# When the first MoE's weight blocks are decoded: a table of four rates in place of three

## The chip, the cores and the metric

One core of a Trainium2 chip runs the whole program. The time is the device time of one execution in microseconds (us), and lower is better. The engines have these names: PE multiplies matrices (PEld is its weight load, which overlaps), DVE is VectorE, ACT is ScalarE, POOL is GpSimd, and SP issues most of the DMAs.

## What is computed

Windowed and dilated causal attention, then two feed-forward layers ("MoE 1" and "MoE 2") with different activations. The weights arrive as float64.

```python
attn_out = _attn_ref(q, k, v)              # B=4, H=8, S=576, D=64; window 32, dilation 4 in half of the heads
x = attn_out.transpose(0, 2, 1, 3).reshape(2304, 512)
# MoE 1: w_in 512x2048, w_out 2048x512
h = x @ w_in
g = np.maximum(h, 0.0) + alpha * np.minimum(h, 0.0)
x = g @ w_out
# MoE 2: its own w_in, w_out
h = x @ w_in
P = a[0] + a[1]*h + a[2]*h*h + a[3]*h*h*h
Q = 1.0 + np.abs(b[0])*np.abs(h) + np.abs(b[1])*h*h
out = (P / (Q + 1e-06)) @ w_out
```

## The kernel before

**Products.** Each operand is split into a high part (`wh`, `xh`) and a low rest (`wl`, `xl`), and each product is three matmuls: wl by xh, wh by xl, wh by xh.

**Steps.** The 2304 tokens are taken in 8 groups `u` of 288, and the 2048 hidden units in 16 blocks `f` of 128. A step of MoE 1 is one pair (u, f), and there are 128. The list `SEQ` gives their order: steps 0 to 7 are group 0 with blocks 0 to 7, steps 8 to 15 group 1 with the same blocks 0 to 7, steps 16 to 23 group 0 with blocks 8 to 15, steps 24 to 31 group 1 with blocks 8 to 15, and from step 32 on one group after the other with all 16 blocks. So steps 8 to 15 need no block that steps 0 to 7 did not need, and step 16 + i needs block 8 + i for the first time.

Step n has two halves (`half1`). The first issues the 12 matmuls of `h` (L520) into one of two banks; the second issues the 12 matmuls of `y` (L673) for step n - 2, which need `w_out` of that step's block. Behind `h` runs a chain: ACT `r` (L640), DVE `h` (L643, the larger of two), ACT `g` high (L646), DVE `g` low (L649). When `g` low is done, the bank is free for `h` of step n + 2. Beside the steps run the attention jobs of the later groups: two load q and k (`tq`, `tk`), transpose them on PE (`pq`, `pk`), which ACT copies out (`qT`, `kT`, L362 and L363), multiply them (`ps`), and then turn and multiply further (`pr`, `pp`, L448).

**Turns.** A turn decodes two float64 pieces into float32: for turn k of MoE 1 these are `w_in` of block k and `w_out` of block k - 2 (turns 0, 1, 16 and 17 have one piece only). There are 18 turns for MoE 1 and 18 for MoE 2. A turn's stages are: `w64_load` (SP, L131 and L136, 512 KB each, two buffers `raw`), `w64_exponent` (ACT L145, one instruction of 128x1024), `w64_sign`, `w64_upper`, `w64_lower` (DVE L151, L158, L164, of 128x1024 each), and for MoE 1 `w64_hi` (ACT L187, makes `wh`) and `w64_lo` (DVE L197, makes `wl`, twice 128x512). A turn of MoE 2 stores its result to DRAM (`w2f`, SP L171) behind `w64_lower` instead. `tick()` runs all stages once, the load being that of the turn after the next. A head ahead of step 0 does the first four turns and one load more.

**The pace.** `half1` begins with

```python
rate = next((r for m, r in PACE if n < m), 0)
pace[0] += rate / 2
while pace[0] >= 1:
    pace[0] -= 1
    tick()
```

so a rate of 0.75 is three turns in four steps. `PACE` is a list of (step at which the rate ends, rate). The code's order is only a priority: a scheduler orders each engine's instructions by it, by what each depends on, and by its own estimates of their costs, and can issue a turn's instructions earlier than its tick.

Of the kernel before, what the change touches and what calls it, by code (L numbers as in the profile page):

```python
# [22 lines left out]
def tile_attention_moe_moe2(  # L23
# [60 lines left out]
    MAN = ''  # L84
    MAN_FROM = 0
    MAN_TO = 128
    PACE = ((14, 0.75), (22, 0.55), (128, 0.23))

    cst = ctx.enter_context(tc.tile_pool(name="cst", bufs=1))
    wpool = ctx.enter_context(tc.tile_pool(name="wpool", bufs=NF))  # L90
# [435 lines left out]
    if True:  # L526
# [225 lines left out]
        def half1(n, half):  # L752
            u = n // NF
            rate = next((r for m, r in PACE if n < m), 0)
            pace[0] += rate / 2
# [223 lines left out]
```

## Time and profile before

| | us |
|---|---|
| median of 3 runs | 977.42 |
| the three runs | 972.84, 977.42, 978.7 |
| the profiled execution | 978.13 |
| its span, first to last instruction | 976.4 |
| PE busy in the span | 937.6 |
| DVE busy | 666.2 |
| ACT busy | 632.1 |
| mean granted clock of PE, share of full speed | 0.979 |

The span is 1.7 us shorter than the execution that was profiled, and that execution is 0.7 us above the median. Busy time is an engine's own work, not its waits.

### The profile page before, as it was taken

To read this page: it belongs to the slowest core of one execution; us is meant where nothing else is said; L and a number is where in the kernel's file an instruction comes from. 1 tells how busy PE (TensorE), PEld (TensorE's weight loads), DVE (VectorE), ACT (ScalarE), POOL (GpSimd) and SP (SyncE) were. 2 spreads that over 40 slices of the span, in tenths; PEclk is the share of its full clock that TensorE was granted. 3 is DMA by queue.
4 is the path that set the end of the run, shared out by engine and by line. 5 is a ranking of instruction groups with operands and counts; after the bars stand their busy time and mean duration, and the time that the engine had idled before them with its cause. 6 is when DMAs were issued, how large, how long until landed. Compare 5 with 4: busy or idle time off the path is not lost.

```text
span 976.4 us, 18434 instructions
## 1 busy us (share of the span) xinstructions
PE 937.6 (96%) x6704; PEld 874.4 (90%) x6704; DVE 666.2 (68%) x1578; ACT 632.1 (65%) x1575; POOL 212.7 (22%) x257
## 2 busy tenths in 40 slices
PE   6789899999999999999999999999999999999998
PEld 5678799889899999999999999999999999999996
DVE  2888885556456555554435679877777788777776
ACT  3876665656455565564545578777677776777765
POOL 2000000001000010000112345434343343343332
PEclk7799999999999999999999999999999999999999
DMA  7656535563634535322134432002030020020000
GB/s 182 162 177 178 201 117 161 137 196 97 188 115 119 184 112 162 124 83 83 50 109 136 153 112 66 1 33 65 1 94 4 31 67 1 33 65 1 34 1 33
DMA packets 93899, 94.41 MB, mean 97 GB/s; under 512 B 40176, under 2 KB 81648, under 8 KB 93808
## 3 DMA queue, kind: packets, MB, share of 16 engines
q1 hardware_dynamic: 87360, 83.78, 28.1%
q0 software_dynamic: 6448, 9.45, 3.8%
q8 instruction: 53, 0.87, 0.4%
q14 instruction: 38, 0.31, 0.1%
HBM read 69.48 MB, written 23.72 MB: 95 GB/s over the span
## 4 chain that ended last, share of the span: by engine, by line
PE 83%; ACT 5%; DMA 5%; DVE 4%; issue 1%; SPq 1%; POOL 0%; POOLq 0%; ACTq 0%; DVEq 0%
PE h L520 39%; PE o L892 20%; PE y L673 17%; DMA raw<-in_moe_w_out_dram 3%; PE px L499 2%; PE pp L448 2%; ACT pr L427 1%; PE ps L405 1%; DMA hd<-in_q_dram 1%; PE ps L393 1%; ACT hd L427 1%; DVE w L158 1%; DVE wl L197 1%; DVE w L164 1%; PE pk L356 1%
## 5 line engine op out<-in xcount | busy, mean ns | idle before, releaser
L520 PE MATMUL h<-x1h,wl 128*128 128x288 f32 x512 | 159.3, 312 | 7.0 <-DVE g_0l L649 2.4
L520 PE MATMUL h<-x1l,wh 128*128 128x288 f32 x512 | 154.2, 301 | 0.0
L520 PE MATMUL h<-x1h,wh 128*128 128x288 f32 x512 | 153.5, 300 | 0.0
L643 DVE SCALAR_TENSOR_TENSOR h<-h,salpha,r 128x288 f32<-128x288 f32 x128 | 66.9, 523 | 112.7 <-ACT r L640 112.6
L520 PE MATMUL h<-x2h,wl 128*128 128x384 f32 x384 | 130.4, 340 | 0.0
L520 PE MATMUL h<-x2h,wh 128*128 128x384 f32 x384 | 130.0, 339 | 0.0
L520 PE MATMUL h<-x2l,wh 128*128 128x384 f32 x384 | 129.6, 338 | 0.0
L640 ACT ACTIVATE r<-h,side 128x288 f32<-128x288 f32 x128 | 63.9, 499 | 98.3 <-PE h L520 98.0
L437 POOL TENSOR_TENSOR pr<-pr,sm 128x480 f32<-128x480 f32 (+2 forms) x20 | 23.9, 1197 | 467.5 <-DVE sm L435 416.8
L520 PEld LDWEIGHTS h<-x1h,wl 128*128 128x128 f32 x512 | 98.2, 192 | 11.2 <-DVE g_0l L649 2.6
L824 POOL TENSOR_SCALAR qq<-hh,babs 128x384 f32<-128x384 f32 x96 | 56.7, 591 | 225.3 <-ACT hh L822 225.2
L827 POOL TENSOR_TENSOR qq<-qq,w 128x384 f32<-128x384 f32 x96 | 97.5, 1016 | 8.3 <-POOL qq L824 0.5
L520 PEld LDWEIGHTS h<-x1h,wh 128*128 128x128 f32 x512 | 98.8, 193 | 0.1
L520 PEld LDWEIGHTS h<-x1l,wh 128*128 128x128 f32 x512 | 98.5, 192 | 0.3 <-DVE x1l L512 0.2
L822 ACT ACTIVATE hh<-h 128x384 f32<-128x384 f32 x96 | 47.2, 492 | 62.7 <-PE h L520 62.7
L829 DVE TENSOR_TENSOR t<-h,t 128x384 f32<-128x384 f32 x96 | 53.5, 557 | 48.1 <-ACT t L828 47.6
L520 PEld LDWEIGHTS h<-x2h,wl 128*128 128x128 f32 x384 | 72.0, 188 | 4.0
L520 PEld LDWEIGHTS h<-x2l,wh 128*128 128x128 f32 x384 | 72.1, 188 | 3.6
L838 ACT ACTIVATE w<-qq 128x384 f32<-128x384 f32 (+1 forms) x98 | 50.8, 519 | 33.5 <-POOL qq L827 33.5
L520 PEld LDWEIGHTS h<-x2h,wh 128*128 128x128 f32 x384 | 72.0, 187 | 0.0
L846 DVE TENSOR_TENSOR qq<-qq,w 128x384 f32<-128x384 f32 (+1 forms) x98 | 54.2, 553 | 24.4 <-ACT w L841 24.1
L427 ACT ACTIVATE pr<-pr,mx 128x96 f32<-128x96 f32 (+2 forms) x182 | 65.1, 360 | 5.9 <-DVE mx L419 5.7
(356 smaller groups left out, 2550.2 us busy)
## 6 DMA issues: line engine op xcount, KB each, us to landing
raw<-in_moe_w_in_dram SPq DMA_DIRECT2D x32, 512.0 KB
raw<-in_moe_w_out_dram SPq DMA_DIRECT2D x32, 512.0 KB
w2f<-w SPq DMA_DIRECT2D x32, 256.0 KB
w<-w2f SPq DMA_DIRECT2D x16, 512.0 KB
x2h<-x2hi POOLq DMA_DIRECT2D x6, 768.0 KB, 5.0
x2l<-x2lo POOLq DMA_DIRECT2D x6, 768.0 KB, 6.3
out_dram<-o SPq DMA_DIRECT2D x15, 256.0 KB
tq<-in_q_dram SPq DMA_DIRECT2D x28, 72.0 KB
```

The costliest lines, as they stand in the source:

```text
L427: nc.scalar.activation(pr[:, j, :], pr[:, j, :], AF.Exp, scale=-1.0, bias=mx[:, j : j + 1], accum_out=sm[:, j : j + 1],)
L520: nc.tensor.matmul(ph[:, :n], lhsT=w_[:, c * P : (c + 1) * P], rhs=x_[:, c, :], start=(i == 0), stop=(i == 3 * KD - 1),)
L640: nc.scalar.activation(r, h, AF.Identity, scale=sg)
L643: nc.vector.scalar_tensor_tensor(h, h, sa, r, op0=ALU.mult, op1=ALU.max)
L673: nc.tensor.matmul(ys[c][:, :C1], lhsT=w_[:, s], rhs=g_, start=begin and i == 0, stop=end and i == 2,)
L822: nc.scalar.activation(hh, h, AF.Square)
L824: nc.gpsimd.tensor_scalar(qq, hh, babs, 1.0 + 1e-6, op0=ALU.mult, op1=ALU.add)
L827: nc.gpsimd.tensor_tensor(qq, qq, w, op=ALU.add)
L829: nc.vector.tensor_tensor(t, h, t, op=ALU.mult)
L838: nc.scalar.activation(w[:, s], qq[:, s], AF.Abs_reciprocal_sqrt, scale=2.0**-44)
L846: nc.vector.tensor_tensor(qq[:, s], qq[:, s], w[:, s], op=ALU.mult)
L892: nc.tensor.matmul(o2[c][i], lhsT=g_, rhs=w_, start=(f == 0 and j == 0), stop=(f == NF - 1 and j == 2),)
```

## The change

One line: the table of rates.

```diff
--- before.py
+++ after.py
@@ -84,7 +84,7 @@
     MAN = ''
     MAN_FROM = 0
     MAN_TO = 128
-    PACE = ((14, 0.75), (22, 0.55), (128, 0.23))
+    PACE = ((8, 0.75), (16, 0.25), (24, 0.75), (128, 0.22))
```

It does two things. In steps 8 to 23 it gives the turns other places: by the program, turn 10 has its tick at step 9 before and 11.5 now, turn 12 at 11.5 and 17, turn 15 at 16.5 and 21, turn 17 at 20 and 23.5 (11.5 is the second half of step 11). From step 24 on it moves every turn of MoE 2: turn 18 from 22 to 28.5, turn 20 from 31 to 37.5, turn 24 from 48 to 55.5, turn 35 from 96 to 105.5. No instruction is added or removed.

How this moves instructions is seen at three places. The first is DVE in steps 11 to 13. Names: `w_12`, `wl_12` belong to turn 12, and `h_1_3`, `g_1_3l` to group 1, block 3, which is step 11. Before:

```order
L151 TENSOR_SCALAR w_12_1264<-raw_1218 128x1024
L197 TENSOR_TENSOR wl_11_1222<-w_11_1214,wh_11_1221 128x512
L197 TENSOR_TENSOR wl_9_1086<-w_11_1214,wh_9_1085 128x512
L158 SCALAR_TENSOR_TENSOR w_12_1264<-raw_1218,w_12_1264 128x1024
L643 SCALAR_TENSOR_TENSOR h_1_3_1247<-h_1_3_1247,salpha,r_1_3_1260 128x288
L164 SCALAR_TENSOR_TENSOR w_12_1264<-raw_1218,w_12_1264 128x1024
L649 SCALAR_TENSOR_TENSOR g_1_3l<-h_1_3_1247,side,g_1_3h 128x288
L643 SCALAR_TENSOR_TENSOR h_1_4_1293<-h_1_4_1293,salpha,r_1_4_1306 128x288
L151 TENSOR_SCALAR w_13_1325<-raw_1268 128x1024
```

And now:

```order
L643 SCALAR_TENSOR_TENSOR h_1_3_1219<-h_1_3_1219,salpha,r_1_3_1232 128x288
L197 TENSOR_TENSOR wl_9_1086<-w_11_1378,wh_9_1085 128x512
L151 TENSOR_SCALAR w_12_1439<-raw_1382 128x1024
L649 SCALAR_TENSOR_TENSOR g_1_3l<-h_1_3_1219,side,g_1_3h 128x288
L158 SCALAR_TENSOR_TENSOR w_12_1439<-raw_1382,w_12_1439 128x1024
L643 SCALAR_TENSOR_TENSOR h_1_4_1265<-h_1_4_1265,salpha,r_1_4_1278 128x288
L164 SCALAR_TENSOR_TENSOR w_12_1439<-raw_1382,w_12_1439 128x1024
L649 SCALAR_TENSOR_TENSOR g_1_4l<-h_1_4_1265,side,g_1_4h 128x288
L643 SCALAR_TENSOR_TENSOR h_1_5_1297<-h_1_5_1297,salpha,r_1_5_1310 128x288
```

Turn 12's last two DVE instructions stood ahead of `g_1_3l` and `h_1_4` and stand behind `g_1_3l` now, so a turn takes one and a half steps there where it took one.

The second is SP's queue around step 27, where group 0's results are stored (`x2lo`) and the attention job 3 of its group is loaded (`tq_3`, `tk_3`, `tv_3`); `raw` are the 512 KB pieces of a turn, `w2f` a decoded piece of MoE 2. Before:

```order
L706 DMA x2lo<-y_0_3l 128x288
L131 DMA raw_2005<-in_moe_w_in_dram 128x4x256
L171 DMA w2f<-w_19_2000 128x512
L136 DMA raw_2005<-in_moe_w_out_dram 128x1024
L296 DMA tq_3_2132<-in_q_dram 72x2x256
L296 DMA tk_3_2133<-in_k_dram 72x2x256
L296 DMA tv_3_2200<-in_v_dram 72x2x256
L131 DMA raw_2318<-in_moe_w_in_dram 128x4x256
L136 DMA raw_2318<-in_moe_w_out_dram 128x1024
```

And now:

```order
L706 DMA x2lo<-y_0_3l 128x288
L131 DMA raw_2121<-in_moe_w_in_dram 128x4x256
L296 DMA tv_3_2191<-in_v_dram 72x2x256
L296 DMA tq_3_2123<-in_q_dram 72x2x256
L296 DMA tk_3_2124<-in_k_dram 72x2x256
L323 DMA tq_0_2235<-in_q_dram 96x3x64
L171 DMA w2f<-w_18_2116 128x512
```

Two 512 KB pieces stood ahead of `tq_3` and two close behind it; one stands ahead of it now, and none directly behind.

The third is ACT at step 36 (group 2, block 4). `raw_2577` is turn 22 before, and `raw_2700` is turn 21 now; `qT_2` and `kT_2` are copies that PE's next attention matmuls wait for. Before:

```order
L640 ACTIVATE r_2_4_2659<-h_2_4_2646,side 128x288
L646 ACTIVATE g_2_4h<-h_2_4_2646,side 128x288
L145 ACTIVATE raw_2577<-raw_2577 128x1024
L640 ACTIVATE r_2_5_2696<-h_2_5_2683,side 128x288
L362 ACTIVATE qT_2_2720<-pq_2_2699 128x288
L363 ACTIVATE kT_2_2719<-pk_2_2700 128x416
L646 ACTIVATE g_2_5h<-h_2_5_2683,side 128x288
```

And now:

```order
L640 ACTIVATE r_2_4_2639<-h_2_4_2626,side 128x288
L145 ACTIVATE raw_2700<-raw_2700 128x1024
L646 ACTIVATE g_2_4h<-h_2_4_2626,side 128x288
L640 ACTIVATE r_2_5_2676<-h_2_5_2663,side 128x288
L362 ACTIVATE qT_2_2710<-pq_2_2679 128x288
L363 ACTIVATE kT_2_2709<-pk_2_2680 128x416
L646 ACTIVATE g_2_5h<-h_2_5_2663,side 128x288
```

A turn is still decoded at this place, another one, and its first instruction stands one place earlier.

## Rows read from the trace of the kernel before

**Rows 1.** The page, busy time of each engine and its share of the span.

```profile
PE 937.6 (96%) x6704; PEld 874.4 (90%) x6704; DVE 666.2 (68%) x1578; ACT 632.1 (65%) x1575; POOL 212.7 (22%) x257
```

**Rows 2.** Busy time by stretch: length, engines (instructions), granted clock, DMA share, GB/s.

```profile
91.62:124.02 32.40, 27.30 (x195) 25.79 (x195) 29.07 (x49) 19.79 (x41) 0.00 (x0) 1.00 0.62 208
124.02:142.68 18.66, 18.66 (x141) 18.66 (x142) 15.41 (x33) 12.39 (x31) 0.00 (x0) 1.00 0.38 117
168.00:172.00 4.00, 3.11 (x24) 2.88 (x22) 2.25 (x19) 3.59 (x18) 0.00 (x0) 1.00 1.05 289
174.00:178.00 4.00, 4.00 (x34) 3.66 (x34) 0.98 (x2) 3.15 (x6) 0.00 (x0) 0.57 0.54 114
270.00:272.50 2.50, 2.50 (x11) 2.29 (x10) 0.52 (x1) 0.62 (x2) 0.00 (x0) 0.50 0.52 164
300.00:560.00 260.00, 258.96 (x2285) 250.77 (x2284) 138.10 (x393) 144.75 (x416) 31.49 (x26) 1.00 0.39 121
```

**Rows 3.** PE's waits, 84 to 160 us: sum, times, longest.

```profile
PE h L520 <- DVE g_5l L649: 1.5, 1, 1.5
PE h L520 <- DVE g_4l L649: 1.0, 1, 1.0
PE h L520 <- DVE g_1l L649: 1.0, 1, 1.0
```

**Rows 4.** PE's timeline: start, length, instruction, and idle time before it with its releaser.

```profile
94.36 0.29 PE L520 MATMUL h<-x1h,wl 128*128 128x288 f32 x1
...
126.77 0.29 PE L520 MATMUL h<-x1h,wl 128*128 128x288 f32 x1
...
129.95 0.29 PE L520 MATMUL h<-x1h,wl 128*128 128x288 f32 x1
...
172.06 0.44 PE L352 MATMUL pq<-ident,tq 72*128 72x72 f32 x4 [0.96 <-DMA tq<-in_q_dram]
...
173.01 0.44 PE L356 MATMUL pk<-ident,tk 72*128 72x72 f32 x4 [0.50 <-DVE g_12l L649]
...
215.49 0.74 PE L448 MATMUL pp<-ident,pr 128*96 128x128 f32 x5 [1.85 <-ACT qT L362]
...
268.35 0.83 PE L448 MATMUL pp<-ident,pr 128*96 128x128 f32 x4 [2.27 <-ACT qT L362]
```

**Rows 5.** DVE's timeline: one turn and the steps' own work between.

```profile
96.75 0.53 DVE L643 SCALAR_TENSOR_TENSOR h<-h,salpha,r 128x288 f32<-128x288 f32 x1 [0.28 <-ACT r L640]
...
103.77 0.69 DVE L151 TENSOR_SCALAR w<-raw 128x1024 int32<-128x1024 int32 x1
104.37 1.28 DVE L197 TENSOR_TENSOR wl<-w,wh 128x512 fp32r<-128x512 f32 x2
105.58 1.22 DVE L158 SCALAR_TENSOR_TENSOR w<-raw,w 128x1024 int32<-128x1024 int32 x1
106.71 0.52 DVE L643 SCALAR_TENSOR_TENSOR h<-h,salpha,r 128x288 f32<-128x288 f32 x1
107.14 1.21 DVE L164 SCALAR_TENSOR_TENSOR w<-raw,w 128x1024 int32<-128x1024 int32 x1
108.27 0.51 DVE L649 SCALAR_TENSOR_TENSOR g_3l<-h,side,g_3h 128x288 fp32r<-128x288 f32 x1
```

**Rows 6.** DVE's waits, 97 to 138 us: sum, times, longest.

```profile
DVE w L151 <- ACT raw L145: 3.3, 4, 1.4
```

**Rows 7.** SP's timeline: start and length of two issues.

```profile
165.60 0.38 SPq L296 DMA_DIRECT2D tq<-in_q_dram  x1
...
259.17 0.57 SPq L136 DMA_DIRECT2D raw<-in_moe_w_out_dram  x1
```

**Rows 8.** ACT's timeline, two of the turns' first instructions.

```profile
213.56 1.10 ACT L145 ACTIVATE raw<-raw 128x1024 f32<-128x1024 f32 x1 [3.62 <-DMA raw<-in_moe_w_out_dram]
...
266.81 1.10 ACT L145 ACTIVATE raw<-raw 128x1024 f32<-128x1024 f32 x1 [3.01 <-DMA raw<-in_moe_w_out_dram]
```

**Rows 9.** ACT's waits, 160 to 560 us: sum, times, longest.

```profile
ACT raw L145 <- DMA raw<-in_moe_w_out_dram: 13.5, 9, 3.6
```

## The prediction

> **What bounds the kernel now.** The page's first part shows PE busy for 937.6 of 976.4 us [rows 1]. So PE is the bound, and a change that adds and removes no instruction can win at most the rest, 38.8 us, and only where PE waits. I read next the busy time in stretches, then PE's list of waits, then the timeline at each wait. From 300 to 560 us PE is busy for 258.96 of 260.00 us [rows 2]: the change moves MoE 2's turns there too, but there is nothing to win, only something to lose. What lies ahead of step 0 is not touched. What is left is steps 8 to 60 (91 to 300 us), with four places at which PE waits:
>
> - Steps 8 to 16. PE is busy for 27.30 us in 32.40, DVE for 29.07, and in the 18.66 us behind that PE is busy all the time [rows 2]. The waits are `h` on DVE's `g` low of two steps before: 1.0, 1.0 and 1.5 us [rows 3], the other waits there are under 1 us each. So DVE is the bound here, and the reader should see why: a turn costs DVE 0.60 + 1.21 + 1.13 + 1.13 = 4.07 us (start to start: L151 103.77 to 104.37, the two L197 to 105.58, L158 to 106.71, L164 107.14 to 108.27) and a step's own L643 and L649 0.86 (0.43 each) [rows 5]. With one turn in each step that makes 4.93 us a step, where PE alone needs 3.18 (126.77 to 129.95 [rows 4]).
> - Step 28, 172 us: 0.96 us on the load of `tq`, 0.50 behind it, and then 4 us at a granted clock of 0.57 [rows 2, 4].
> - Step 37, 215 us: 1.85 us on `qT` [rows 4].
> - Step 49, 268 us: 2.27 us on `qT`, and then 2.5 us at the lower of the clock's two levels, 0.50 [rows 2, 4].
>
> **Term 1: steps 8 to 24.** From step 9's `h` (94.36) to step 17's (126.77) are 32.41 us [rows 4]; eight steps that wait for nothing take 8 x 3.18 = 25.44. So at most 6.9 us are to be had here. This is more than the sum of the listed waits, since PE also starts up slowly behind each.
>
> The change moves the turns of these steps back, and by the order turns 12 to 17 stand half a step to two steps later. Do they meet what needs them? Block 8 + i's `w_in` is needed at step 16 + i, its `w_out` two steps later, and by the order each `wl` stands two to three steps of DVE's row ahead of its use. So the weights are no new wait by themselves. The question is whether DVE's work fits into PE's unstalled pace up to step 22, where the denser turns end. I count what DVE does now between the larger of step 9, which ends near 97.2 (96.75 + 0.43 [rows 5]), and the `g` low that step 22 needs, by the order of the changed kernel: five turns of full size and two of one piece, 23 instructions of L643 and L649, 13 of L197. For the half-sized instructions I take 0.35 (L151) and 0.60 (L158, L164), about half of the full ones and a little more. L151: 5 x 0.60 + 2 x 0.35 = 3.7. L158: 5 x 1.13 + 2 x 0.60 = 6.9. L164: one half-sized less, 6.3. L197: 13 x 0.605 = 7.9. The steps' own: 23 x 0.43 = 9.9. The attention job's maxima, estimated as two instructions of that size: 0.9. Sum 35.5 us, so DVE could end at 132.7. PE, if it never waits, starts step 22 at 94.36 + 13 x 3.18 = 135.7. The spare is 3.0 us. DVE cannot use all of it, because it waits for ACT's L145, and that for loads: in the same stretch of the kernel before these waits were 3.3 us [rows 6]. It just fits or just misses. Walking the two engines by hand through the order I find no wait at steps 11 to 17 (`h` of step 11 near 101.8) and one of about a microsecond at step 22. So I take -6.9 + 1.0 = **-5.9 us**, with 0 and -6.9 as its ends.
>
> **Term 2: step 28.** SP issues `tq` at 165.60 [rows 7], between the 512 KB pieces of two turns, and the DMA engines are full from 168 to 172 (share 1.05 [rows 2]). In the changed order one piece stands ahead of it and none directly behind. So `tq` should land in time. Its price was 0.96 + 0.50 of idle time and 4 x (1 - 0.57) = 1.7 for the clock, which fell behind the wait: **-3.2 us** (ends 0 and -3.2).
>
> **Term 3: step 37.** ACT's L145 of turn 22 waits 3.62 us for its piece [rows 8]; `qT`, which PE needs, stands behind it in ACT's queue, and PE pays 1.85. In the changed order turn 21 is decoded there, one instruction earlier on ACT, with a load that has no other turn's right behind it. With 0.15 for the start-up: **-2.0 us** (ends 0 and -2.0).
>
> **Term 4: step 49.** The same pattern: L145 of turn 26 waits 3.01 [rows 8], `qT` is behind it. It costs 2.27, some 0.25 for the start-up, and 2.5 x (1 - 0.50) = 1.25 for the clock, 3.8 us. The changed order has no L145 at this place, but it has the same row (`g` high, L145, `qT`) at step 65, where the L164 that frees the load's buffer stands as close ahead as here. I take **0**, with -3.8 and 0 as ends.
>
> **Term 5: new waits of MoE 2's turns.** The turns come in gaps of two to six steps of PE in both kernels, because the scheduler pulls them forward. A gap of two steps is about 8 us there, and a load took 7.64 from its issue (259.17) to ACT's start (266.81) [rows 7, 8]. So a turn two steps behind the last makes ACT wait. ACT waited nine times for 13.5 us in all from 160 to 560 [rows 9], and of these only the two of terms 3 and 4 reached PE. The changed order has about as many such gaps as the old one, and a new one at step 34 (turn 20), for which I estimate an ACT wait of 2.3 us, of which PE pays 0.5. For the rest I take one more at half of the price of step 37's. Together **+1.5 us**; the ends are 0 and, with two like step 49's less what is gone, +6.
>
> Here a page would give another answer. The Trainium skill, "DMA: Bandwidth & Descriptors", section "Anatomy of one DMA — SWDGE (gpsimd) path", has the fit 2.0 us + bytes / 436e3 for one DMA; by it a piece of 512 KB would take an estimated 3.2 us and a turn's pair 4.4. This trace shows 7.64 for SP's queue, so the trace decides, but by the page the waits at steps 34 and 65 would not be there, which is rival B below.
>
> **The sum.** Terms 2 and 3 depend on where the scheduler's order meets the DMAs, so I take two thirds of their 5.2: -3.4. Then -5.9 - 3.4 + 0 + 1.5 = -7.8 us. From the profiled 978.13 that is 970.3, and on the median, 0.7 lower, **969.5 us**. The three runs of before differ by 5.9 us; I take 1% (9.8 us) as what a measurement can tell from no change, so the forecast is inside "no change", at its edge.
>
> **Rivals.**
>
> A. *The wait moves to steps 16 to 24.* DVE has 3.0 us spare up to step 22. For: the 3.3 us that it waited for L145 in this stretch before [rows 6], as much as the spare; denser turns from step 17 on. Against: those waits came in a row of turns at one per step, and the first of the new turns has its load long before. One load 3 us later than needed gives back 3 us, two give back the whole term; I price it at 4.5, 969.5 + 4.5 = 974.
>
> B. *All loads come in time.* Then all four waits go, with 0.5 us of new ones: -6.9 - 3.2 - 2.0 - 3.8 + 0.5 = -15.4, or 962 us. For: the turns of MoE 2 are a little rarer by the table. Against: the two-step gaps are still there, and ACT waited in them.
>
> C. *Slower: MoE 2's turns stall PE.* Each two-step gap whose L145 stands ahead of a `qT` costs PE what step 49's did, 3.8 to 4.1 us with the fall of the clock. Both kernels have some six such gaps, of which two hit a `qT` before. If four more hit one now, that is +16.4, against -11.1 for terms 1 to 3: +5.3, or 983 us. It decides from three on. Against: only two hits in 18 turns so far.
>
> D. *The change does not do what it says.* The scheduler ignores the table where a turn can go earlier; the order shows that turn 12 moves only by a step. If DVE is as dense as before between 94 and 127 us, term 1 is near 0, and what terms 2 and 3 give is taken back by term 5: 977.
>
> **How the numbers follow.** Forecast (965 to 973.5) 0.52, A (971 to 977) 0.17, B (960.5 to 965) 0.14, C (978 to 990) 0.09, D (975 to 979) 0.08. The range goes from 962, in the middle of B, to 978.5, the upper end of D: left out are half of B and nearly all of C, 0.07 + 0.08, and a little of D. Faster by over 1% means below 967.6: B, and a quarter of the forecast's own, 0.14 + 0.14 = 0.28. Slower by over 1% means above 987.2: 0.04, the far half of C. The rest, 0.68, is within 1%.
>
> **What would show it.** Right: in the changed profile PE is busy for all but a microsecond from 94 us to step 22, which starts near 136; no wait of `h` on `g` low in steps 9 to 16; DVE's busy share lower there and near 0.9 from step 17 to 23; no `tq` wait at step 28 and no clock of 0.57 behind it. Wrong: waits of PE on `wl` (L197) or on `g` low in steps 17 to 24; a wait of `pp` on `qT` behind an L145 that waits for a load, at steps 34 to 65 or later, with a fall of the clock behind it. The steps that I trust least are the two thirds of terms 2 and 3, which rest on an order and not on a trace, and the 3.0 us of spare.

## The result and the profile after

The changed kernel takes 965.24 us (median of 4 runs, 964.16 to 967.78) against 977.03 (4 runs): a ratio of 0.9889, 95% interval 0.9852 to 0.9927. Its profiled execution took 964.16 us, 13.97 less than that of the kernel before. Of those, PE's own busy time gives 4.7 (part of it the slow clock), the rest are waits that are gone. All of the interval is faster than before; the gain on the medians is 1.2%. The page's first part of the changed kernel:

```profile
PE 932.9 (97%) x6704; PEld 871.2 (91%) x6704; DVE 666.0 (69%) x1578; ACT 630.1 (65%) x1575; POOL 213.2 (22%) x257
```

Its busy time by stretch (columns as in [rows 2]; the first stretch is steps 9 to 16; behind it the changed kernel is ahead of the old one in time, so that a stretch holds slightly later work):

```profile
94.48:120.70 26.22, 25.70 (x194) 25.47 (x193) 24.01 (x38) 17.08 (x32) 0.00 (x0) 1.00 0.65 215
...
168.00:172.00 4.00, 4.00 (x43) 3.76 (x42) 2.26 (x18) 3.17 (x13) 0.00 (x0) 1.00 0.81 227
174.00:178.00 4.00, 4.00 (x38) 3.98 (x38) 1.98 (x4) 1.85 (x6) 0.00 (x0) 1.00 0.27 61
...
300.00:560.00 260.00, 259.09 (x2253) 251.31 (x2252) 144.65 (x391) 147.02 (x412) 36.00 (x31) 1.00 0.42 131
```

The same eight steps in the kernel before:

```profile
94.36:126.77 32.41, 27.31 (x196) 25.80 (x195) 29.11 (x49) 20.71 (x42) 0.00 (x0) 1.00 0.55 192
```

In these steps DVE now has 24.01 us of work for 29.11, about a turn and a quarter less, and PE is busy for all but half a microsecond, where 5.1 us of the old stretch were idle. The share of DVE's busy time did not fall with it (0.92 for 0.90), because the steps became as much shorter. The clock is full from 168 to 172 and from 174 to 178 us. Behind 300 us next to nothing has changed. PE's timeline of the changed kernel at the places of [rows 4]:

```profile
94.48 0.29 PE L520 MATMUL h<-x1h,wl 128*128 128x288 f32 x1
...
102.05 0.40 PE L520 MATMUL h<-x1h,wl 128*128 128x288 f32 x1 [0.52 <-DVE g_1l L649]
...
120.70 0.29 PE L520 MATMUL h<-x1h,wl 128*128 128x288 f32 x1
...
205.72 0.74 PE L448 MATMUL pp<-ident,pr 128*96 128x128 f32 x5 [0.26 <-ACT qT L362]
...
319.92 0.85 PE L448 MATMUL pp<-ident,pr 128*96 128x128 f32 x4 [0.25 <-ACT qT L362]
```

Step 9 to step 17 takes 94.48 to 120.70, 26.22 us for 32.41, with one wait of 0.52. At step 37 `pp` waits 0.26 for 1.85, and at step 65, where the pattern of step 49 now stands, 0.25 for 2.27.

**A ledger by steps.** From each trace I took the start of the first matmul of `y` with `g` low in a step, by which a step can be named in every kernel here. The table has the length of five stretches, as the difference to the profile of the kernel before, whose own lengths are in the first line (us):

```
               9->22   28->30   36->40   50->52   52->126
before         48.85    12.53    18.83    13.28    282.22
changed        -5.38    -3.07    -1.88    -4.00     -0.36
```

The sum is -14.7; with the other steps it is the -13.97 of the two executions.

### The profile page after: what moved, and what is told of

It reads as the page before. It is cut to its first block, busy times and chain, and to the rows that moved or that the text cites. A ratio compares the mean times of both kernels' runs of the same rounds, so it can differ in the third digit from the quotient of the medians.

```text
span 962.4 us, 18434 instructions
## 1 busy us (share of the span) xinstructions
PE 932.9 (97%) x6704; PEld 871.2 (91%) x6704; DVE 666.0 (69%) x1578; ACT 630.1 (65%) x1575; POOL 213.2 (22%) x257
## 4 chain that ended last, share of the span: by engine, by line
PE 81%; DMA 6%; ACT 5%; DVE 4%; issue 1%; SPq 1%; POOL 0%; POOLq 0%; ACTq 0%; DVEq 0%
PE h L520 38%; PE o L892 20%; PE y L673 16%; DMA raw<-in_moe_w_out_dram 4%; PE px L499 2%; PE pp L448 1%; PE ps L405 1%; ACT pr L427 1%; DMA hd<-in_q_dram 1%; PE ps L393 1%; DVE w L158 1%; ACT raw L145 1%; ACT hd L427 1%; PE pk L356 1%; DVE wl L197 1%
## 5 line engine op out<-in xcount | busy, mean ns | idle before, releaser
L643 DVE SCALAR_TENSOR_TENSOR h<-h,salpha,r 128x288 f32<-128x288 f32 x128 | 66.9, 523 | 97.8 <-ACT r L640 97.5
```

Of the source, the lines that this page charges most:

```text
L643: nc.vector.scalar_tensor_tensor(h, h, sa, r, op0=ALU.mult, op1=ALU.max)
```

## The experiments

The four kernels that move turns (`early`, `late` with its copy, `two`, `t20`) name the half-steps of the ticks instead of a rate:

```diff
-            rate = next((r for m, r in PACE if n < m), 0)
-            pace[0] += rate / 2
-            while pace[0] >= 1:
-                pace[0] -= 1
+            for _ in range(TICKS.count(2 * n + half)):
                 tick()
```

The ledger of all kernels that ran, in the columns of the one above (each line is one profiled execution; those down to `nolo` have the old order in steps 9 to 22 or behind them, or in both):

```
               9->22   28->30   36->40   50->52   52->126
again          -1.47    -1.83    -0.83    -2.17     +1.24
early          -5.28    -1.08    -2.31    -0.52     +0.97
late           -1.16    -3.07    -2.16    -4.00     -0.60
late2          -1.49    -2.83    -1.98    -3.99     -0.34
two            +0.52    -3.07    +0.40    -4.04     +2.02
t20            -1.08    -2.44    -2.31    -0.24     +0.33
b_pool         -0.11    -2.47    -0.42    -3.46     +0.59
nolo           -3.77    +0.12    -0.60    -3.67     -0.05
after2         -5.87    -3.06    -2.31    -3.98     +0.69
a_nolo         -5.05    -3.06    -2.31    -4.00     -0.07
half           -3.71    -3.01    -2.31    -4.00     -0.46
tail25         -5.58    -2.82    -1.62    -3.38     +1.37
```

**The old kernel again** (`again`, no edit).

> The kernel before, unchanged, to see how much of its stalls at 172, 215 and 268 us belongs to the code and how much to one execution. Theory 1 (the order sets the stalls): the waits of steps 9 to 16 stand as they stood (step 9's h to step 17's in 32.4 us), and so do the three later ones, each within 1 us of its 3.2, 2.0 and 3.8 us. Theory 2 (the load's own time scatters, and a stall is an accident of one execution): steps 9 to 16 stand as they stood, but at least one of the three later ones, above all that at 268 us with its load of 7.64 us, is gone or less than half, and the span is 2 us or more off the 976.4.

Ratio 0.9974 (0.9946 to 1.0001). All the stalls are there, and each is smaller, that of steps 9 to 22 by 1.47 us too, which neither theory had. `qT` at step 49 costs PE 1.59 us of idle time for 2.27, with the clock at 1.00 behind it; at step 28 `pq` waits 0.65 us for DVE and not for `tq`. By the marks that were set, theory 2 came: step 49 at less than half (1.8 for 4.0), the span 3.6 us off. But no stall went altogether, so both theories have a part: the order makes the stall, and the execution sets its size. The first profile of before was a heavy one.

**The two halves of the change** (`early`: `TICKS` of the changed table up to turn 17, of the old one from turn 19; `late`: the other way round).

> Turns 4 to 17 at the steps of the changed table, turns 19 to 35 at those of the old one (turn 18 at step 24, behind turn 17). Theory 1 (each term has its place): only the stalls of steps 9 to 16 go, 5.3 us less, about 971.7 us; tq's wait at step 28 and qT's at steps 37 and 49 are still there. Rival (the later stalls hang on what came before them): they go too, and the time is that of the changed kernel, 965.

> Turns 4 to 17 at the steps of the old table, turns 18 to 35 at those of the changed one. Theory 1: the waits on g low in steps 9 to 16 stand (32.4 us for eight steps), the three later stalls go, 5 to 9 us less, 968 to 972. Rival: the early turns carry the whole gain, and this one is at 976 to 977.

`early` 0.9949 (0.9929 to 0.9970), 970.36 us; `late` 0.9908 (0.9877 to 0.9938), 966.41. In the ledger each does what its place says: `early` has the -5.3 in steps 9 to 22 and keeps the stalls of steps 28 (`tq` waits 1.00 us) and 49, `late` has the old waits and none of the three later stalls; its 966.41 lies below the 968 to 972 of its theory. `early` lost the stall of step 37, though nothing there was changed: the second piece of that load was issued 1.1 us earlier in the step than in the kernel before, and L145 started 6.38 us behind it for 8.14. PE's timeline and the stretches of `early` at step 49, with the price of a long wait:

```profile
260.59 1.06 PE L448 MATMUL pp<-ident,pr 128*96 128x128 f32 x4 [2.22 <-ACT qT L362]
```

```profile
256.00:260.00 4.00, 2.38 (x21) 2.14 (x19) 0.70 (x2) 1.03 (x2) 0.00 (x0) 1.00 0.66 232
260.00:264.00 4.00, 3.41 (x16) 3.26 (x17) 1.83 (x4) 2.70 (x8) 0.00 (x0) 0.57 0.47 146
```

From 260 to 264 us, with the end of the wait of 2.22 us in it, the granted clock was 0.57 in the mean, which is another 1.7 us; the four us behind are at 1.00 again.

**Do the halves add up?** The medians of `early` and `late`, -5.2 and -9.2, make more than the -11.8 of the change, so the changed kernel and `late` ran again on one chip (`after2`, `late2`, no edits).

> The changed kernel, unchanged, beside late2 on one chip. Early turns alone gave 5.2 us and late turns alone 9.2 on the medians; the changed kernel gave 11.8 in other runs. Theory 1 (the terms are apart, so they add): 961 to 963 us here, 3 to 5 us below late2. Rival (they overlap: what the early steps save is waited away later): within 1.5 us of late2.

> Late turns alone once more, beside after2. Theory 1: 3 to 5 us above after2, the difference made in steps 9 to 17 (32.4 us for eight steps here, 26.2 in the changed kernel). Rival: the same time as after2.

`after2` 964.23 us, ratio 0.9884 (0.9853 to 0.9916); `late2` 968.88, 0.9924 (0.9897 to 0.9950). The difference, 4.65 us, is the early half, and the product of 0.9949 and 0.9924 is 0.9873. The halves add, if not to the 961 to 963 of the theory. The profiled execution of `late` had been lucky: at step 9 it was already 1.9 us ahead of the profile of before, that of `late2` 2.4 behind, with the same code up to there.

**DVE or the loads in steps 9 to 16?** In `b_pool` the subtraction of turns 9 to 14 goes to POOL:

```diff
-    RAWB = 2
+    RAWB = 2; LO0, LO1 = 9, 15
...
-                nc.vector.tensor_tensor(
+                (nc.gpsimd if LO0 <= n < LO1 else nc.vector).tensor_tensor(
                     wl[1, f][:, s], t[:, i * DM : (i + 1) * DM],
```

> The old table, with L197 (the low part) of turns 9 to 14 on POOL instead of DVE, which has nothing to do there. Is it DVE that bounds steps 9 to 16, or the loads that its turns wait for? Theory 1 (DVE): a turn costs DVE 2.86 instead of 4.07 us, a step with one turn 3.72 instead of 4.93; eight steps take 28 to 30 us instead of 32.4, 2.5 to 4.5 less in all. Rival (loads): DVE only waits longer for L145, and the eight steps stay above 31.5 us. POOL's subtraction may take longer than DVE's; if PE then waits on wl, that shows as a wait on POOL.

Ratio 0.9977 (0.9960 to 0.9994), and -0.11 in steps 9 to 22: nothing gained there; the eight steps took 31.65 us, as the rival had it. That is not the rival's proof, since DVE was not relieved. DVE's groups by line from 92 to 125 us, of `b_pool` and then of the kernel before (count, busy us, mean ns):

```profile
L158 DVE SCALAR_TENSOR_TENSOR w<-raw,w 128x1024 int32<-128x1024 int32 x5 | 8.9, 1789 | 0.1
...
L151 DVE TENSOR_SCALAR w<-raw 128x1024 int32<-128x1024 int32 x5 | 4.6, 917 | 2.3 <-ACT raw L145 2.1 <-issue 0.2
L643 DVE SCALAR_TENSOR_TENSOR h<-h,salpha,r 128x288 f32<-128x288 f32 x8 | 4.1, 514 | 0.0
```

```profile
L158 DVE SCALAR_TENSOR_TENSOR w<-raw,w 128x1024 int32<-128x1024 int32 x6 | 7.3, 1218 | 0.0
...
L643 DVE SCALAR_TENSOR_TENSOR h<-h,salpha,r 128x288 f32<-128x288 f32 x8 | 4.2, 520 | 0.3 <-ACT r L640 0.3
L151 DVE TENSOR_SCALAR w<-raw 128x1024 int32<-128x1024 int32 x6 | 4.1, 688 | 3.0 <-ACT raw L145 3.0
```

With POOL at work beside it, DVE's L158 takes 1789 ns on average for 1218, L164 1684 for 1214 and L151 917 for 688; L643, whose `h` is in PSUM, keeps its time (514 for 520). The averages mix two kinds: the L158 that meet a subtraction take 2.1 to 2.2 us, the others 1.2. What POOL took over, it took back from the others.

So the work was left out instead (`nolo`, on the old table; `a_nolo`, on the changed one):

```diff
-        wl[moe, f] = wpool.tile([P, 2 * DM], F32R, tag="wl", name=f"wl{moe}_{f}")
+        wl[moe, f] = wh[moe, f] if moe == 1 and 8 <= f < 14 else wpool.tile([P, 2 * DM], F32R, tag="wl", name=f"wl{moe}_{f}")
...
-                nc.vector.tensor_tensor(
+                8 <= f < 14 or nc.vector.tensor_tensor(
                     wl[1, f][:, s], t[:, i * DM : (i + 1) * DM],
```

> The old table, but the low parts of blocks 8 to 13 are not made (12 of the L197, 0.605 us each, go from DVE in turns 8 to 15); PE multiplies by the high part instead, so it has as many matmuls, and the low part's product is left out of the result. Theory 1 (DVE bounds steps 9 to 16): a step with a turn costs DVE 3.7 instead of 4.9 us, the eight steps take 27 to 30 us instead of 31 to 32.4. Rival (the loads bound them): DVE waits longer for L145 and the eight steps stay at 31 or more.

> The changed table, with the low parts of blocks 8 to 13 left out as in nolo. Theory 1 (in the changed kernel DVE no longer bounds steps 9 to 24): steps 9 to 22 take as long as in the changed kernel within 0.6 us, the wait that it still has on g low. Rival (DVE is still the bound there, at its 3 us of spare): 1 to 3 us less.

`nolo` 0.9926 (0.9900 to 0.9952), 968.41 us; the eight steps take 28.4 us, and steps 9 to 22 are 3.77 us shorter than in the profile of before, 2.3 shorter than in `again`. In these steps no `h` waits for `g` low any more, though DVE still waited 2.3 us for L145: what made PE wait was DVE's own work. The 1.6 us that `nolo` is behind the changed kernel there are mostly other things: 18 `ps` matmuls of an attention job now stand in steps 10, 16 and 17 (in the kernel before they are done ahead of step 9, in 1.03 us), and PE waits 0.68 us for a copy of `yp` (L691). `a_nolo`, on the changed table, took 963.75 us in one run, and its steps 9 to 22 are as long as those of the two profiles of the changed kernel (-5.05 beside -5.38 and -5.87), with 18 more `ps` in step 19, which is 0.67 us longer. Less work on DVE wins nothing there: DVE no longer bounds these steps.

**Which neighbours make the late stalls?** `two` is the old order with turn 24 two steps earlier (its old tick is at 48.5; the section on the change has 48) and turn 19 two steps later; `t20` moves turn 20 alone. The first line of each cut is the old table's ticks written out, which the kernel before makes from its rates; numbers that stay are left out.

```diff
-    TICKS = (2, 5, ..., 44, 53, 62, 70, 79, 88, 97, 105, ..., 253)
+    TICKS = (2, 5, ..., 44, 57, 62, 70, 79, 88, 93, 105, ..., 253)
```

```diff
-    TICKS = (2, 5, ..., 44, 53, 62, 70, 79, 88, 97, 105, ..., 253)
+    TICKS = (2, 5, ..., 44, 53, 67, 70, 79, 88, 97, 105, ..., 253)
```

> The old table with two turns moved, each at one late stall: turn 24 two steps earlier (tick 46.5 for 48.5), so that the load that L145 of turn 26 waits for at step 49 is issued two steps earlier, and L145 stands three rows ahead of qT instead of right ahead of it; turn 19 two steps later (tick 28.5 for 26.5), so that two pieces of 512 KB still stand ahead of tq_3, and none behind it. Theory 1 (the stall at step 49 is the load's lateness, the one at step 28 the pieces ahead of tq): no wait for qT at step 49, 1.8 to 4 us less from there on; tq's wait at step 28 still there. Rival (the pieces behind tq share the DMA engines with it): the wait at step 28 goes or halves, 1.5 to 3 us. If neither stall moves, the turns' places don't set them.

> The old table with turn 20 alone moved, from step 31 to 33.5. In SP's queue the row up to tq_3 is the old one (a piece of 512 KB, a store of w2f, a piece, tq_3, tk_3, tv_3), but the next two pieces no longer follow behind tv_3. The run of two turns left open whether the stall at step 28 went with the pieces behind tq or with the store between the pieces. If the pieces behind (theory now): no wait on tq, and step 28 to 29 is 1.5 to 3 us shorter than in the kernel before. If what stands ahead: the wait is there as it was.

`two` 0.9962 (0.9931 to 0.9993): the stall of step 49 is gone (-4.04), and so is that of step 28 (-3.07), against my theory of the pieces ahead. On the medians that is 1.7 us and not 7, since other executions of the old order stall less than the first profile. `t20` in one run: step 28 shorter by 2.44, step 49 as it was (-0.24). SP's queue of `t20` around `tq`:

```profile
163.55 0.45 SPq L131 DMA_DIRECT2D raw<-in_moe_w_in_dram  x1
164.96 0.32 SPq L171 DMA_DIRECT2D w2f<-w  x1
165.33 0.42 SPq L136 DMA_DIRECT2D raw<-in_moe_w_out_dram  x1
165.85 0.37 SPq L296 DMA_DIRECT2D tq<-in_q_dram  x1
166.31 0.35 SPq L296 DMA_DIRECT2D tk<-in_k_dram  x1
166.71 0.40 SPq L296 DMA_DIRECT2D tv<-in_v_dram  x1
167.17 0.40 SPq L682 DMA_DIRECT2D yp<-y1p  x1
```

The row ahead of `tq` is the old one, and `pq` started at 171.24, 5.39 us behind the issue, without a wait on `tq`. Five executions have the two pieces right behind. In three of them PE had to wait for `tq`, until 6.46 us behind its issue (before), 6.41 (`early`) and 6.66 (`nolo`); in `again` `pq` started at 6.16, held by DVE, and in `b_pool` at 5.54 without a wait. In the nine without the pieces behind, two of which (`two`, `t20`) have both pieces ahead, PE never waited for `tq`. So the pieces ahead don't make the wait. It came only with pieces issued behind, but not each time, and `t20` ran once: that they hold `tq` up is likely, and not shown.

In `two` L145 at step 37 waited 4.28 us for its load, longer than before, and PE paid 2.51, with the clock at 1.00 behind it.

**Other tables** (`tail25`: 0.25 for 0.22 from step 24; `half`: `((8, 0.75), (24, 0.5), (128, 0.22))`).

> The changed table with 0.25 in the place of 0.22 from step 24 on. In ACT's row an L145 stands right ahead of a qT at steps 36, 49, 65 and 81 (in the changed kernel only at step 65). Theory 1 (a stall needs both, an L145 ahead of qT and its load issued no more than two steps earlier): the load is issued two steps ahead at step 36 and three at 49, 65 and 81, so one stall of 1 to 2 us at step 36 and none at the others, 1 to 2 us above the changed kernel. Rival (the place ahead of qT is enough): four stalls of 1 to 4 us, 6 us or more above it. Second rival (only the rate counts): the same time as the changed kernel.

> The changed table with a rate of 0.5 from step 8 to 24 instead of 0.25 and then 0.75. Theory 1 (DVE bounds only where a step's share of a turn and its own work pass PE's 3.18 us): 0.5 x 4.07 + 0.86 = 2.9 us, so no more waits than in the changed kernel, 963 to 966 us. Rival (the turns must be out of steps 8 to 16): the waits on g low come back there in part, 966 to 969.

`tail25` 0.9929 (0.9901 to 0.9956), 968.33 us; `half` 0.9903 (0.9866 to 0.9940), 966.32. None of the expectations of `tail25` came: L145 at step 36 waited 1.76 us, but no `pp` waited for `qT` anywhere, so being ahead of `qT` behind a recent load is not enough either. What counts is when L145 starts. Counted from the ledger's mark of step 36, it started at 3.48 us here and PE paid nothing; at 4.37 (`again`), 4.56 (`b_pool`), 4.61 (`nolo`), 5.34 (before) and 6.01 (`two`) PE paid 0.90, 1.08, 1.14, 1.85 and 2.51, each time the start less 3.5. An L145 that waits, but starts before that, is free. The profile of `tail25` is 1.7 us behind that of `after2` at step 9; the other 2.7 of its difference of 4.4 are spread over small ones, 0.7 at most in a column, that I have not taken apart. `half` saves 3.71 in steps 9 to 22 for 5.4 to 5.9, of which a wait of 1.3 on the store's copy (`yp`, L691) is the most; its interval overlaps that of the changed kernel, so it can't be told from it. Its `h` waits for `g` low are 0.2 us at most, as its theory had it, though the time is just above the theory's 963 to 966. No table here beat the changed one.

## Why the prediction was right, and where its sum was off

The time lies in the range and on the side that was forecast; the forecast itself, -7.8 us, was too small against -11.8 (interval -7.1 to -14.5), and against -13.97 in the profiled executions. The range was 16.5 us wide, and what came, faster by over 1%, had been given 0.28 against 0.68 for a time within 1%: the range was kept by its width as much as by the sum.

- **Term 1** (-5.9): -5.38 and -5.87 in the two profiles of the changed kernel, and -4.65 to -5.2 on the medians, since other executions of the old order mostly lose less there than the profile that I read (1.1 to 1.5 us less in four, 0.5 more in `two`). The bound was DVE's density, as argued: `nolo` and `a_nolo` show it. Two details were wrong: DVE's busy share in steps 9 to 16 was to be lower and is 0.92 for 0.90, and no wait appeared at step 22. Some 0.8 us did come back between steps 17 and 24, of which 0.40 are two `ps` matmuls that PE now does behind step 17.
- **Term 2** (-3.2, counted at two thirds): -3.07. The cause was named half rightly: not the pieces ahead of `tq` (`two`, `t20`), and probably those behind it. The fall of the clock in its price came in two executions only (before, `nolo`); the old order cost 0.6 to 3.2 us here in five profiles.
- **Term 3** (-2.0, counted at two thirds): -1.88 and -2.31. The load is not in time here, though. L145 of turn 21 still waits for it:

```profile
203.36 1.14 ACT L145 ACTIVATE raw<-raw 128x1024 f32<-128x1024 f32 x1 [2.70 <-DMA raw<-in_moe_w_out_dram]
```

In six executions with the changed order it waits 1.6 to 2.7 us, and PE pays 0.26 at most. The second piece is issued 1.2 us earlier in the step than in the kernel before and L145 starts 7.29 us behind it for 8.14, so that it starts 3.33 us behind the mark of step 36 for 5.34. Its place one instruction earlier on ACT did not help by itself: `qT` starts 1.80 us behind L145 now, and 1.38 before.
- **Term 4** (0): the largest miss of the sum: -4.00 and -3.98. I had argued that step 65 would pay the same again. The pattern did come back there: L164, the two issues and L145 follow each other as at step 49, SP's issue at 312.67 for 259.17 and ACT's start at 318.36 for 266.81:

```profile
318.36 1.13 ACT L145 ACTIVATE raw<-raw 128x1024 f32<-128x1024 f32 x1 [1.03 <-DMA raw<-in_moe_w_out_dram]
```

But the load took 5.69 us for 7.64, and PE paid 0.25. This is no single lucky execution. The starts of L145 (us behind the ledger's mark of the step) and PE's waits for `qT` behind it:

```
step 49   before  early   t20  again  b_pool   nolo      step 65    half  after2  changed  a_nolo  late2   late
start       5.65   5.59  5.61   4.97    3.64   3.45                 3.69    3.67     3.65    3.41   3.37   3.29
PE waits    2.27   2.22  2.23   1.59    0.29   0.09                 0.29    0.26     0.25    0.01   0.00   0.00
```

The loads are issued at the same place in all twelve (2.0 us ahead of the mark); they took 5.3 to 5.7 us in each of the six at step 65, and 7.6, 7.6, 7.6, 7.0, 5.6 and 5.4 at step 49. PE's wait is the start less 3.4. So the old order's stall was not 4.0 every time: in the ledger it is 1.8 (`again`), 3.5 (`early`), 3.8 (`t20`), 0.5 and 0.3 (`b_pool`, `nolo`). A mean of these and the first profile is 2.3.
- **Term 5** (+1.5): -0.36 and +0.69 in steps 52 to 126, and +0.6 in both between steps 30 and 50 outside the columns. The new wait that was named did not come: L145 of turn 20, at step 34, waited 0.08 us (2.3 estimated). ACT waited for loads about as much as before, 12.1 us in 8 waits for 13.5 in 9 [rows 9].

So the time lies between the forecast and rival B's 962, and B's result came, no wait of more than 0.52 us left of the four stalls, but not its mechanism: the loads are not in time, they are only early enough for PE. The price of a load by the Trainium skill, an estimated 4.4 us for a pair ("DMA: Bandwidth & Descriptors", section "Anatomy of one DMA — SWDGE (gpsimd) path"), is for DMAs that gpsimd issues, and these loads are issued by SP; here it is too low: the pair at step 65 took 5.69 us from its second issue to its use. Rivals A, C and D did not happen: no wait on `g` low or `wl` from step 17 to 24, no stall of over a microsecond behind step 17, and the order did what the table says.

What stays open: why the same load behind the same issues takes 5.4 us once and 7.6 another time, whether and how pieces issued later delay an earlier one, and what shifts the start of step 9 by up to 4.3 us between executions of the same head (-1.93 to +2.39). The DMA packets in the traces narrow the first: of the 128 packets of 4 KB of the second piece at steps 49 and 65, the first 120 have ended 4.5 to 5.4 us behind the issue in all twelve executions; the last eight end at 7.1 us in before, `early` and `t20`, at 6.5 in `again`, and at 4.9 to 5.2 in the others. So it is one sixteenth of the piece that comes late.

## What to carry to other kernels

Work that is done ahead of its need is not free where an engine's share of it in a step, added to that engine's fixed work of the step, is more than the step of the engine that bounds the kernel: 4.07 and 0.86 against 3.18 us here. Spread it until the sum fits, and check that each piece is still ready when it is needed. A wait on a load costs only when the bound engine needs something that stands behind the waiting instruction, and then only what is later than that need; so read the time of the need, and not the length of the wait. A single profile gives the price of such a stall badly: take several executions of the same code before pricing it, above all for a case that is expected to repeat elsewhere. When two halves of a change are to be added, run both beside the whole on one chip.

## What was not expected of the hardware

POOL's subtraction of two SBUF tensors slowed DVE's L158 and L164 by 47 and 39% in the mean, while DVE's instruction with an operand in PSUM kept its time (the rows of `b_pool` above). The Trainium skill, "SBUF — State Buffer", section "🔬 SBUF: two separate sides", says that DVE and GpSimd share a port pair that one of them locks for a whole instruction, where DVE has two SBUF inputs or runs in a two-port mode. The rows agree for L158 and L164, which have two SBUF inputs, and for L643. L151 has one SBUF input and rose by a third too (917 for 688 ns); it takes 688 ns where L158 takes 1218 for as many elements, which would fit such a mode, but no run shows that it was in one.
